# Summing keys and values over eight tokens by accumulating transfers, in a pooled-attention and gated feed-forward kernel

## The chip, the cores and the metric

The kernel runs on one core of a Trainium2 chip. The metric is the device time of one execution in microseconds, the median of three runs; lower is better. Five engines matter here: TensorE (PE, with its weight loads as PEld), VectorE (DVE), ScalarE (ACT), GpSimd (POOL) and the queue of SyncE (SP), from which the kernel before issues all its transfers.

## The reference

Inputs q, k, v are 8 batches x 8 heads x 576 tokens x 64. Keys and values are averaged over groups of eight tokens, so that 72 pooled keys and values remain for each head. Attention over them is followed by a gated feed-forward block on the 4608 tokens.

```python
k_p = k.reshape(B, H, Sp, pool, D).mean(axis=3)        # Sp = 72, pool = 8
v_p = v.reshape(B, H, Sp, pool, D).mean(axis=3)
scores = scale * np.matmul(q, k_p.transpose(0, 1, 3, 2))
scores = scores - np.max(scores, axis=-1, keepdims=True)
attn = np.exp(scores)
attn = attn / (np.sum(attn, axis=-1, keepdims=True) + 1e-09)
attn_out = np.matmul(attn, v_p)
x = attn_out.transpose(0, 2, 1, 3).reshape(B * S, H * D)   # 4608 x 512
out = ((x @ w_a) * (x @ w_b)) @ w_out                      # d_ff = 1536
```

## The kernel before

Every product is made of three matmuls on a high and a low part of its operands (`hi x hi + hi x lo + lo x hi`). ACT makes the high part by a rounding copy, and DVE or POOL the low part by a subtraction (`low_part`, line 182). So the feed-forward block alone has 9 token tiles x 12 slices of d_ff x 36 matmuls of 128x512.

The order of all work is written out when the program is built. The list `order` of `in` slices (`ffn_in`: 24 matmuls into psa and psb) and `out` slices (`ffn_out`: 12 matmuls into acc) is the backbone. Everything else runs in chains (Python generators) that `Chains.step` resumes: once in six backbone matmuls the clock of the chains moves by one step, and a chain that says `yield n` goes on n steps later. Each engine then executes its instructions strictly in the order in which the chains issued them, and waits for what the next one needs. Before the first backbone matmul, and wherever `need` is called, the steps go by without matmuls, so there they are no measure of time.

The chains: `load_keys(b)` and `load_values(b)` make the pooled keys `kdiag` and values `vdiag`, `vrem` of batch b; `chunk(i)` takes 128 (or 64) tokens through scores (`psc`), softmax (`s`, `m`, `z`), the split of the probabilities (`pr`, `rem`), their transposes (`ptr`) and the product with the values (`po`), which ends as `xh`, `xl`, the input of the backbone; `convert_weights` turns the float64 words of the three weight matrices into float32 (ACT lines 224 and 225, DVE lines 226, 230 and 235, with one area of loaded words for each matrix); `split_weight` makes the parts `jha/jla`, `jhb/jlb`, `jho/jlo` of a weight slice, in two buffers each; `gated` multiplies psa's copy `h` with psb (line 556) and splits the product into `hh`, `hl`.

In `load_keys` of batches 1 to 7 four transfers of 128x576 come on SP's queue, two at a time into two buffers, and four DVE reductions (line 281) sum groups of eight neighbours into `kp`, two after each pair of loads. ACT scales a pair into the high part of `kdiag` (line 292) and DVE makes its low part (line 297). `load_values` does the same with four transfers of 128x512 and two of 96x512 and six reductions (line 333) into `vp`; then come `vwide` (line 342), the low part of `vdiag` (line 356) and that of `vrem`. Batch 0 uses other buffers, loaded at the very start. POOL's work is the low parts of most weight slices and of the probabilities, and the division of the exponentials (line 457).

Of the kernel before, what the change touches and what calls it, by code (L numbers as in the profile page):

```python
# [9 lines left out]
F32 = mybir.dt.float32  # L10
# [16 lines left out]
NK = DM // P  # L27
# [19 lines left out]
NR = 3 * 4 * KR  # L47
NG = H // 4
# [70 lines left out]


@with_exitstack
def attn_moe_kernel(ctx: ExitStack, tc: tile.TileContext, q, k, v, vr, wa, wb, wo, out):
    nc = tc.nc
    const = ctx.enter_context(tc.tile_pool(name="const", bufs=1))
    sb = ctx.enter_context(tc.tile_pool(name="sb", bufs=2))
# [55 lines left out]
    def low_part(eng, lo, src, hi):  # L181
        eng.tensor_tensor(out=lo, in0=src, in1=hi.bitcast(F32), op=ALU.subtract)  # L182
# [72 lines left out]
    def split_weight(name, x):  # L255
# [7 lines left out]
        low_part(nc.vector if x < NF and name != "o" else nc.gpsimd, lo, raw[name][:, f, :], hi)  # L263
        parts[name, x] = hi, lo

    def load_keys(b):
        kd = kdiag[b % 2]
        kp = tmp(f"kp_{b}")[:, :NK * SP].rearrange("p (g s) -> p g s", g=NK)
        for g0 in range(0, NK, 2):
            gs = slice(g0, g0 + 2)  # L270
            if b == 0:
                kraw = [early_k[:, g, :] for g in (g0, g0 + 1)]
            else:
                if g0:
                    yield from wait(("kraw", b, 0))
                kraw = [sb.tile([P, S], F32, tag="kv", name=f"kraw_{b}_{g}") for g in (g0, g0 + 1)]
                for j in range(2):
                    nc.sync.dma_start(kraw[j], k[b, :, g0 + j, :])
                yield 4
            for j in range(2):  # L280
                nc.vector.tensor_reduce(
                    out=kp[:, g0 + j, :],
                    in_=kraw[j].rearrange("p (s j) -> p s j", j=POOL),
                    axis=AX.X,
                    op=ALU.add,
                )
                if b:
                    yield 1
            mark("kraw", b, g0)
            for e in range(2):  # L290
                r = slice(e * D, e * D + D)
                nc.scalar.mul(kd[r, gs, 0, e, :], kp[r, gs], 1.0 / POOL)
            if b:
                yield 1
            for e in range(2):
                r = slice(e * D, e * D + D)
                nc.vector.scalar_tensor_tensor(
                    out=kd[r, gs, 1, e, :],
                    in0=kp[r, gs],
                    scalar=1.0 / POOL,  # L300
                    in1=kd[r, gs, 0, e, :].bitcast(F32),
                    op0=ALU.mult,
                    op1=ALU.subtract,
                )
            mark("keys", b, g0)

    def load_values(b):
        vd = vdiag[b % 2]
        vrem = sb.tile([P, NG, 2, 2, D], F32R, tag="vrem", name=f"vrem_{b}")
        yield from wait(("keys", b, 2), ("values", b - 1))  # L310
        vp = sb.tile([P, NK + NG, D], F32, tag="vp", name=f"vp_{b}", bufs=1)
        for x0 in range(0, NK + NG, 2):
            if b == 0:
                vraw = [early_v[:, x, :] if x < NK else early_vr[:, x - NK, :] for x in (x0, x0 + 1)]
            else:
                if x0:
                    yield from wait(("vraw", b, x0 - 2))
                vraw = [sb.tile([P, S], F32, tag="kv", name=f"vraw_{b}_{x0 + j}")[:, :D * POOL] for j in range(2)]
                for j in range(2):
# [5 lines left out]
            for j in range(2):
                x, rows = x0 + j, P if x0 < NK else NR
                vv = vraw[j][:rows].rearrange("p (d j) -> p d j", j=POOL)
                if b == 0 and 0 < x < NK:
                    for n in (4, 2, 1):
                        to = vp[:rows, x].unsqueeze(2) if n == 1 else vv[:, :, :n]  # L330
                        nc.gpsimd.tensor_tensor(out=to, in0=vv[:, :, :n], in1=vv[:, :, n:2 * n], op=ALU.add)
                else:
                    nc.vector.tensor_reduce(out=vp[:rows, x], in_=vv, axis=AX.X, op=ALU.add)
            mark("vraw", b, x0)
            yield 1
        for e in range(2):
            r = slice(e * KM, e * KM + KM)
            nc.scalar.mul(vd[r, :, 0, r], vp[r, :NK], 1.0 / POOL)

        wide = tmp(f"vwide_{b}").rearrange("p (r j e d) -> p r (j e) d", r=NG, j=2, e=2)  # L340
        for r in range(NG):
            nc.vector.scalar_tensor_tensor(
                out=wide[:NR, r],
                in0=vp[:NR, NK + r].unsqueeze(1).broadcast_to([NR, 4, D]),
                scalar=1.0 / POOL,
                in1=mask[:NR].unsqueeze(2).broadcast_to([NR, 4, D]),
                op0=ALU.mult,
                op1=ALU.mult,
            )
        wide = wide.rearrange("p r c d -> p (r c d)")  # L350
        vrf = vrem.rearrange("p r j e d -> p (r j e d)")
        yield 1
        nc.scalar.copy(vrf[:NR], wide[:NR])
        for e in range(2):
            r = slice(e * KM, e * KM + KM)
            nc.vector.scalar_tensor_tensor(
                out=vd[r, :, 1, r],
                in0=vp[r, :NK],
                scalar=1.0 / POOL,
                in1=vd[r, :, 0, r].bitcast(F32),  # L360
                op0=ALU.mult,
                op1=ALU.subtract,
            )
# [298 lines left out]
    for kind, t, f, *_ in order:  # L662
        x = t * NF + f
# [7 lines left out]
    with tc.manual_schedule():  # L671
        load_early()
        nc.vector.tensor_copy(ident, ident0)
        for t in kdiag + vdiag:
            nc.gpsimd.memset(t.bitcast(F32), 0.0)
        nc.vector.tensor_reduce(
            out=mask[:NR], in_=ident0[:NR, :NR].rearrange("p (a c s) -> p c a s", a=3, c=4), axis=AX.XY, op=ALU.add
        )
        chains.start(load_keys(0), KEYS)
        for i in range(early):  # L680
            chains.start(chunk(i), (CHUNKS[0], i), EARLY_GAP * i)
        for i in range(early, sum(t < 2 for t in tile_of)):
# [16 lines left out]
        for n, (kind, t, f, *_) in enumerate(order):  # L699
            x = t * NF + f  # L700
# [82 lines left out]
```

## Time and profile before

| | us |
|---|---|
| median of the three runs | 1086.49 (1084.5 to 1088.29) |
| the profiled execution | 1083.36 |
| its span, first to last instruction | 1081.6 |
| PE busy in the span | 1032.1 (95%) |
| DVE busy | 585.9 (54%) |
| ACT busy | 515.6 (48%) |
| POOL busy | 506.6 (47%) |
| mean share of the DMA engines on SP's queue | 18.1% |

The profiled execution is 3.1 us faster than the median of the runs. The busy shares are means over two very different stages: a start of about 135 us, in which the first chunks and the first weight slices are made, and the long rest, in which the backbone runs. A busy PE in this profile includes matmuls that overlap, so 95% does not say that the array works at its peak.

### The profile page before, as it was taken

Reading aid. Unit: us, or ns where it says so; the run is one execution under the profiler, and the core shown is the slowest. Engines: PE = TensorE matmul, PEld = TensorE weight load, DVE = VectorE, ACT = ScalarE, POOL = GpSimd, SP = SyncE. Lnnn points to the kernel's source line nnn. Section 1 sums busy time; section 2 is a strip of 40 time slices with the busy share of each in tenths; the row PEclk is TensorE's granted clock in tenths of the full one; section 3 lists DMA queues with packets and bytes.
Section 4 is the critical chain, followed back from the end, with each engine's and each line's share of the span. In section 5 each row is a group of like instructions: output and inputs, shape, how many; then the busy total and the mean of one; then the engine's idle time right before and its main releaser. Section 6 shows DMA issues by size and latency. Waiting matters only on the chain.

```text
span 1081.6 us, 13576 instructions
## 1 busy us (share of the span) xinstructions
PE 1032.1 (95%) x4964; PEld 855.9 (79%) x4964; DVE 585.9 (54%) x941; ACT 515.6 (48%) x1035; POOL 506.6 (47%) x425
## 2 busy tenths in 40 slices
PE   4569999999999999999999999999999999999998
PEld 4457788788878888888877888888887888888886
DVE  8879967845784347534575437543567344322112
ACT  4656645454554445444544445444543444443332
POOL 6322200055565555555546545554545455554442
PEclk9769999999999999999999999999999999999999
DMA  6335445221330004000320003100220010001001
GB/s 221 105 120 157 147 137 170 93 90 50 115 110 1 1 23 140 14 1 1 96 90 1 1 5 106 45 1 1 93 83 1 1 59 1 1 1 39 1 1 39
DMA packets 32178, 63.79 MB, mean 59 GB/s; under 512 B 7376, under 2 KB 7376, under 8 KB 32112
## 3 DMA queue, kind: packets, MB, share of 16 engines
q1 hardware_dynamic: 32112, 62.93, 18.1%
q8 instruction: 39, 0.64, 0.3%
q14 instruction: 27, 0.22, 0.1%
HBM read 51.38 MB, written 11.53 MB: 58 GB/s over the span
## 4 chain that ended last, share of the span: by engine, by line
PE 85%; DVE 9%; ACT 3%; issue 2%; DMA 1%; POOL 0%; DVEq 0%; ACTq 0%; POOLq 0%
PE psb L599 9%; PE psa L599 9%; PE acc L621 9%; PE psb L601 9%; PE psb L600 8%; PE psa L601 8%; PE psa L600 8%; PE acc L623 8%; PE acc L622 8%; PE ptr L502 2%; PE psc L431 2%; PE psc L417 1%; PE po L539 1%; PE po L540 1%; PE po L538 1%
## 5 line engine op out<-in xcount | busy, mean ns | idle before, releaser
L556 DVE TENSOR_TENSOR h<-psb,h 128x512 f32<-128x512 f32 x108 | 74.6, 691 | 318.7 <-PE psb L601 312.8
L182 POOL TENSOR_TENSOR jlb<-wb_raw,jhb 128x512 fp32r<-128x512 f32 x88 | 115.1, 1307 | 254.6 <-ACT jhb L261 254.6
L182 POOL TENSOR_TENSOR jlo<-wo_raw,jho 128x512 fp32r<-128x512 f32 x108 | 143.1, 1325 | 122.5 <-ACT jho L261 122.5
L606 ACT COPY h<-psa 128x512 f32<-128x512 f32 x108 | 63.5, 588 | 251.8 <-PE psa L601 239.8
L599 PE MATMUL psa<-xh,jha 128*128 128x512 f32 x432 | 173.7, 402 | 0.0
L599 PE MATMUL psb<-xh,jhb 128*128 128x512 f32 x432 | 172.0, 398 | 0.8 <-DVE h L556 0.8
L621 PE MATMUL acc<-jho,hh 128*128 128x512 f32 x432 | 171.6, 397 | 0.0
L600 PE MATMUL psa<-xl,jha 128*128 128x512 f32 x432 | 169.4, 392 | 0.7 <-DVE xl L182 0.7
L601 PE MATMUL psa<-xh,jla 128*128 128x512 f32 x432 | 169.7, 393 | 0.4 <-DVE jla L182 0.4
L601 PE MATMUL psb<-xh,jlb 128*128 128x512 f32 x432 | 168.8, 391 | 0.0
L600 PE MATMUL psb<-xl,jhb 128*128 128x512 f32 x432 | 168.7, 391 | 0.0
L623 PE MATMUL acc<-jho,hl 128*128 128x512 f32 x432 | 168.6, 390 | 0.0
L622 PE MATMUL acc<-jlo,hh 128*128 128x512 f32 x432 | 168.2, 389 | 0.0
L182 POOL TENSOR_TENSOR jla<-wa_raw,jha 128x512 fp32r<-128x512 f32 x88 | 120.6, 1371 | 73.9 <-ACT jha L261 66.6
L182 DVE TENSOR_TENSOR hl<-h,hh 128x512 fp32r<-128x512 f32 x100 | 92.7, 927 | 33.5 <-ACT hh L569 33.3
L569 ACT CAST hh<-h 128x512 fp32r<-128x512 f32 x100 | 62.2, 622 | 95.1 <-DVE h L556 92.5
L601 PEld LDWEIGHTS psa<-xh,jla 128*128 128x128 f32 x432 | 81.8, 189 | 18.5 <-DVE jla L182 0.8
L601 PEld LDWEIGHTS psb<-xh,jlb 128*128 128x128 f32 x432 | 81.2, 188 | 17.4
L623 PEld LDWEIGHTS acc<-jho,hl 128*128 128x128 f32 x432 | 81.1, 188 | 17.5
L599 PEld LDWEIGHTS psb<-xh,jhb 128*128 128x128 f32 x432 | 81.3, 188 | 16.4 <-DVE h L556 1.2
L600 PEld LDWEIGHTS psa<-xl,jha 128*128 128x128 f32 x432 | 82.0, 190 | 15.6 <-DVE xl L182 1.1
L599 PEld LDWEIGHTS psa<-xh,jha 128*128 128x128 f32 x432 | 81.7, 189 | 14.8
(93 smaller groups left out, 1693.4 us busy)
## 6 DMA issues: line engine op xcount, KB each, us to landing
out<-y SPq DMA_DIRECT2D x36, 256.0 KB, 2.2
kraw<-in_k SPq DMA_DIRECT2D x28, 288.0 KB, 4.1
qraw<-in_q SPq DMA_DIRECT2D x28, 256.0 KB, 3.7
vraw<-in_v SPq DMA_DIRECT2D x28, 256.0 KB, 3.1
words<-in_wa SPq DMA_DIRECT2D x12, 512.0 KB, 3.6
words<-in_wb SPq DMA_DIRECT2D x12, 512.0 KB, 3.5
words<-in_wo SPq DMA_DIRECT2D x12, 512.0 KB, 3.6
vraw<-in_vr SPq DMA_DIRECT2D x14, 192.0 KB, 2.6
```

Source lines behind the costliest of these rows:

```text
L182: eng.tensor_tensor(out=lo, in0=src, in1=hi.bitcast(F32), op=ALU.subtract)
L431: nc.tensor.matmul(pt[:n, :2 * hk], qh[:, g, :n], kd[:, g].rearrange("p w e s -> p (w e s)"), start=True, stop=False)
L502: nc.tensor.transpose(ptr[:rows, g, :n], src, ident[:n, :n])
L556: nc.vector.tensor_tensor(out=h, in0=pt, in1=h, op=ALU.mult)
L569: nc.scalar.copy(hh, h)
L599: nc.tensor.matmul(pt, wh[:, c], xh[:, kk], start=(kk == 0), stop=False)
L600: nc.tensor.matmul(pt, wh[:, c], xl[:, kk], start=False, stop=False)
L601: nc.tensor.matmul(pt, wl[:, c], xh[:, kk], start=False, stop=(kk == NK - 1))
L606: nc.scalar.copy(h, pt)
L621: nc.tensor.matmul(acc[c], hh[:, cs], wh, start=first, stop=False)
L622: nc.tensor.matmul(acc[c], hh[:, cs], wl, start=False, stop=False)
L623: nc.tensor.matmul(acc[c], hl[:, cs], wh, start=False, stop=last)
```

## The change

Keys and values of batches 1 to 7 are laid out on the host as four pieces with two summands side by side in each row: `kj` has pieces of 128 x 2 x 288 and `vj` of 128 x 2 x 384 (the last two head groups of the values padded with zeros to 128 rows). One plain transfer on SP's queue brings the first piece. Three transfers issued from POOL's queue add the other three to it on their way into the same tile, each three steps after the one before it. Each of them waits until the one before has landed. One DVE addition then sums the two halves. The reductions, the small tiles, `vp` and the shared load buffers `kv` go; `kraw` and `vraw` become one tile each. `load_values` no longer waits for the keys before it begins to load, and its work behind the sum stands elsewhere by some steps. The high and low parts of the keys are made for all four head groups at once. `load_keys(1)` starts at step 4 and not 8.

```diff
+GATHER_FIRST, GATHER = 3, 3
-EARLY_GAP, VALUES_START, KEYS_START, WEIGHTS_START, CONVERT_AFTER = 1, 2, 8, 10, 5
+EARLY_GAP, VALUES_START, KEYS_START, WEIGHTS_START, CONVERT_AFTER = 1, 2, 4, 10, 5
...
+    def gather(dst, src, apart):
+        nc.sync.dma_start(dst, src[0])
+        for x in range(1, POOL // 2):
+            yield apart
+            nc.gpsimd.dma_start(dst, src[x], accum_op=ALU.add)
+        yield apart
+        nc.vector.tensor_tensor(out=dst[:, 0], in0=dst[:, 0], in1=dst[:, 1], op=ALU.add)
...
     def load_keys(b):
...
+            yield from wait(("keys", b - 1, 2))
+            kraw = sb.tile([P, 2, NK * SP], F32, tag="kraw", name=f"kraw_{b}", bufs=1)
+            yield from gather(kraw, kj[b - 1].rearrange("x p (j c) -> x p j c", j=2), GATHER_FIRST if b == 1 else GATHER)
+            kp = kraw[:, 0].rearrange("p (g s) -> p g s", g=NK)
...
-                kraw = [sb.tile([P, S], F32, tag="kv", name=f"kraw_{b}_{g}") for g in (g0, g0 + 1)]
-                for j in range(2):
-                    nc.sync.dma_start(kraw[j], k[b, :, g0 + j, :])
-                yield 4
-            for j in range(2):
-                nc.vector.tensor_reduce(out=kp[:, g0 + j, :], ...)
...
     def load_values(b):
-        yield from wait(("keys", b, 2), ("values", b - 1))
+        yield from wait(("values", b - 1))
+        vraw = sb.tile([P, 2, (NK + NG) * D], F32, tag="vraw", name=f"vraw_{b}", bufs=1)
+        vp = vraw[:, 0].rearrange("p (x d) -> p x d", d=D)
+            yield from gather(vraw, vj[b - 1].rearrange("x p (j c) -> x p j c", j=2), GATHER_FIRST if b == 1 else GATHER)
...
-                    if x0 < NK:
-                        nc.sync.dma_start(vraw[j], v[b, :, x0 + j, :])
-                    else:
-                        nc.sync.dma_start(vraw[j][:NR], vr[b, :, x0 + j - NK, :])
-                yield 3
...
+        yield from wait(("keys", b, 2))
```

TensorE's instructions stand in the same order before and after, without an exception. The order moves on DVE, ACT, POOL and SP. Three places follow.

DVE in the start, from the first chunks' division to the first chunk of batch 1; `kp`, `kraw` and `kdiag_76` belong to the keys of batch 1, `wa` and `wb` to the first weight slices. Before:

```order
L281 TENSOR_REDUCE kp_219<-kraw_0_220 128x72
L457 TENSOR_TENSOR s_235<-s_235,z_237 128x576
L281 TENSOR_REDUCE kp_219<-kraw_1_221 128x72
L226 TENSOR_SCALAR wa_raw<-wa_raw 128x512
L297 SCALAR_TENSOR_TENSOR kdiag_76<-kp_219,kdiag_76 64x2x72 x2
L230 SCALAR_TENSOR_TENSOR wa_raw<-words,wa_raw 128x512
L235 ISA wa_raw<-wa_raw,wlow_a_332 128x1024
L182 TENSOR_TENSOR xl_343<-po_0_349,xh_342 128x2x256
```

And now, with the sum of the keys (line 275) behind the conversion of the first slice; the sum of the values follows some fifteen rows later:

```order
L459 TENSOR_TENSOR s_234<-s_234,z_236 128x576
L228 TENSOR_SCALAR wa_raw<-wa_raw 128x512
L232 SCALAR_TENSOR_TENSOR wa_raw<-words,wa_raw 128x512
L237 ISA wa_raw<-wa_raw,wlow_a_331 128x1024
L275 TENSOR_TENSOR kraw_170<-kraw_170 128x288
L184 TENSOR_TENSOR xl_337<-po_0_344,xh_336 128x2x256
```

Two reductions and a pair of `kdiag` rows are gone from in front of the first conversion, and an addition that needs the third accumulating transfer stands behind it.

POOL in the start, from the split of the first chunks' queries (`ql`) to the first chunk of batch 1 (`s_395`). Before:

```order
L182 TENSOR_TENSOR ql_187<-wa_raw,qh_186 128x512
L182 TENSOR_TENSOR pr_202<-s_120,pr_202 128x512
L182 TENSOR_TENSOR rem_203<-s_120,rem_203 128x2x32
L182 TENSOR_TENSOR pr_211<-s_139,pr_211 128x512
L182 TENSOR_TENSOR rem_212<-s_139,rem_212 128x2x32
L457 TENSOR_TENSOR s_216<-s_216,z_218 128x576
L182 TENSOR_TENSOR pr_304<-s_216,pr_304 128x512
L182 TENSOR_TENSOR rem_305<-s_216,rem_305 128x2x32
L182 TENSOR_TENSOR pr_327<-s_235,pr_327 128x512
```

And now:

```order
L273 DMA kraw_170<-in_kj 128x576
L184 TENSOR_TENSOR pr_205<-s_120,pr_205 128x512
L184 TENSOR_TENSOR rem_206<-s_120,rem_206 128x2x32
L184 TENSOR_TENSOR pr_215<-s_139,pr_215 128x512
L184 TENSOR_TENSOR rem_216<-s_139,rem_216 128x2x32
L273 DMA kraw_170<-in_kj 128x576
L459 TENSOR_TENSOR s_220<-s_220,z_222 128x576
L273 DMA vraw_237<-in_vj 128x768
L273 DMA kraw_170<-in_kj 128x576
L184 TENSOR_TENSOR pr_305<-s_220,pr_305 128x512
L184 TENSOR_TENSOR rem_306<-s_220,rem_306 128x2x32
L273 DMA vraw_237<-in_vj 128x768
```

Six accumulating transfers stand between the splits of the first four chunks' probabilities (the last `vraw` follows behind the fourth chunk's), and each holds what is behind it on POOL until the one before it of the same tile has landed.

DVE in the long stage, where the values of batch 5 meet a chunk's scores (`s` from `psc`, line 437); the same pattern returns at batch 7. Before:

```order
L333 TENSOR_REDUCE vp_5007<-vraw_4_5137 96x64
L333 TENSOR_REDUCE vp_5007<-vraw_5_5138 96x64
L342 SCALAR_TENSOR_TENSOR vwide_5190<-vp_5007,mask 96x256 x2
L556 TENSOR_TENSOR h_5171<-psb_3_5173,h_5171 128x512
L356 SCALAR_TENSOR_TENSOR vdiag_78<-vp_5007,vdiag_78 64x4x64 x2
L182 TENSOR_TENSOR vrem_5006<-vwide_5190,vrem_5006 32x512
L437 TENSOR_REDUCE s_5185<-psc_0_5237 64x144
L437 TENSOR_REDUCE s_5185<-psc_1_5241 64x144
L182 TENSOR_TENSOR hl_5232<-h_5171,hh_5231 128x512
```

And now:

```order
L275 TENSOR_TENSOR vraw_4900<-vraw_4900 128x384
L558 TENSOR_TENSOR h_5052<-psb_3_5054,h_5052 128x512
L344 SCALAR_TENSOR_TENSOR vwide_5089<-vraw_4900,mask 96x256 x2
L358 SCALAR_TENSOR_TENSOR vdiag_78<-vraw_4900,vdiag_78 64x4x64 x2
L439 TENSOR_REDUCE s_5064<-psc_0_5116 64x144
L439 TENSOR_REDUCE s_5064<-psc_1_5120 64x144
L184 TENSOR_TENSOR hl_5109<-h_5052,hh_5108 128x512
L184 TENSOR_TENSOR vrem_4899<-vwide_5089,vrem_4899 32x512
```

The low part of `vrem` went from in front of the first scores to behind them, and two reductions became one addition. At the values of batch 3 the two `vdiag` rows moved in the same way, from between the two pairs of scores to behind both.

More of the change, by code (lines that the diff above doesn't have):

```diff
@@ L121, in attn_moe_kernel @@
 @with_exitstack
-def attn_moe_kernel(ctx: ExitStack, tc: tile.TileContext, q, k, v, vr, wa, wb, wo, out):
+def attn_moe_kernel(ctx: ExitStack, tc: tile.TileContext, q, k, v, vr, kj, vj, wa, wb, wo, out):
     nc = tc.nc
@@ L264, in split_weight @@
         parts[name, x] = hi, lo
+    def gather(dst, src, apart):
[5 more added lines that the diff above has]
+        nc.vector.tensor_tensor(out=dst[:, 0], in0=dst[:, 0], in1=dst[:, 1], op=ALU.add)
     def load_keys(b):
         kd = kdiag[b % 2]
-        kp = tmp(f"kp_{b}")[:, :NK * SP].rearrange("p (g s) -> p g s", g=NK)
-        for g0 in range(0, NK, 2):
-            gs = slice(g0, g0 + 2)
-            if b == 0:
-                kraw = [early_k[:, g, :] for g in (g0, g0 + 1)]
-            else:
-                if g0:
-                    yield from wait(("kraw", b, 0))
-                kraw = [sb.tile([P, S], F32, tag="kv", name=f"kraw_{b}_{g}") for g in (g0, g0 + 1)]
-                for j in range(2):
-                    nc.sync.dma_start(kraw[j], k[b, :, g0 + j, :])
-                yield 4
-            for j in range(2):
[L281 to L289, printed above, removed]
+        if b == 0:
+            kp = tmp(f"kp_{b}")[:, :NK * SP].rearrange("p (g s) -> p g s", g=NK)
+        else:
+            yield from wait(("keys", b - 1, 2))
+            kraw = sb.tile([P, 2, NK * SP], F32, tag="kraw", name=f"kraw_{b}", bufs=1)
+            yield from gather(kraw, kj[b - 1].rearrange("x p (j c) -> x p j c", j=2), GATHER_FIRST if b == 1 else GATHER)
+            kp = kraw[:, 0].rearrange("p (g s) -> p g s", g=NK)
+            yield 1
+        many = 2 if b == 0 else NK
+        for g0 in range(0, NK, many):
+            gs = slice(g0, g0 + many)
+            if b == 0:
+                for g in range(g0, g0 + many):
+                    nc.vector.tensor_reduce(
+                        out=kp[:, g, :],
+                        in_=early_k[:, g, :].rearrange("p (s j) -> p s j", j=POOL),
+                        axis=AX.X,
+                        op=ALU.add,
+                    )
             for e in range(2):
@@ L304, in load_keys @@
                 )
-            mark("keys", b, g0)
+            for g in range(g0, g0 + many, 2):
+                mark("keys", b, g)
     def load_values(b):
@@ L309, in load_values @@
         vrem = sb.tile([P, NG, 2, 2, D], F32R, tag="vrem", name=f"vrem_{b}")
-        yield from wait(("keys", b, 2), ("values", b - 1))
[L311 to L319, printed above, removed]
-                    if x0 < NK:
-                        nc.sync.dma_start(vraw[j], v[b, :, x0 + j, :])
-                    else:
-                        nc.sync.dma_start(vraw[j][:NR], vr[b, :, x0 + j - NK, :])
-                yield 3
[L325 to L328, printed above, removed]
+        yield from wait(("values", b - 1))
+        vraw = sb.tile([P, 2, (NK + NG) * D], F32, tag="vraw", name=f"vraw_{b}", bufs=1)
+        vp = vraw[:, 0].rearrange("p (x d) -> p x d", d=D)
+        if b:
+            yield from gather(vraw, vj[b - 1].rearrange("x p (j c) -> x p j c", j=2), GATHER_FIRST if b == 1 else GATHER)
+            yield 1
+        else:
+            for x in range(NK + NG):
+                vv = (early_v[:, x, :] if x < NK else early_vr[:NR, x - NK, :]).rearrange("p (d j) -> p d j", j=POOL)
+                rows = P if x < NK else NR
+                if 0 < x < NK:
                     for n in (4, 2, 1):
@@ L333, in load_values @@
                     nc.vector.tensor_reduce(out=vp[:rows, x], in_=vv, axis=AX.X, op=ALU.add)
-            mark("vraw", b, x0)
-            yield 1
+                if x % 2:
+                    yield 1
+        yield from wait(("keys", b, 2))
         for e in range(2):
@@ L761 @@
     vrl = np.ascontiguousarray(np.repeat(vrl, 3, axis=1).reshape(B, NR, NG, D * POOL))
+    kj = kl[1:].reshape(B - 1, P, NK, SP, POOL // 2, 2).transpose(0, 4, 1, 5, 2, 3)
+    kj = np.ascontiguousarray(kj.reshape(B - 1, POOL // 2, P, 2 * NK * SP))
+    vj = np.zeros((B - 1, P, NK + NG, D, POOL), v.dtype)
+    vj[:, :, :NK] = vl[1:].reshape(B - 1, P, NK, D, POOL)
+    vj[:, :NR, NK:] = vrl[1:].reshape(B - 1, NR, NG, D, POOL)
+    vj = vj.reshape(B - 1, P, NK + NG, D, POOL // 2, 2).transpose(0, 4, 1, 5, 2, 3)
+    vj = np.ascontiguousarray(vj.reshape(B - 1, POOL // 2, P, 2 * (NK + NG) * D))
     wl = {
@@ L769 @@
     wol = np.ascontiguousarray(inputs["moe_w_out"].reshape(NF, P, DM).transpose(1, 0, 2)).view(np.int64)
-    host = {"q": ql, "k": kl, "v": vl, "vr": vrl, "wa": wl["a"], "wb": wl["b"], "wo": wol}
+    host = {"q": ql, "k": kl[:1], "v": vl[:1], "vr": vrl[:1], "kj": kj, "vj": vj, "wa": wl["a"], "wb": wl["b"], "wo": wol}
     nc = bacc.Bacc("TRN2", target_bir_lowering=False, num_devices=1, dynamic_dma_scratch_size=2048)
```

## Prediction

> **What bounds the kernel now.** I read the page first, then the busy time by stretches, then who waits for whom on TensorE, and last the chain and the timelines of the places found. The page's first line, and the stretches; columns there: length, PE busy (count), PEld, DVE, ACT, POOL, granted clock, DMA share, GB/s.
>
> ```profile
> span 1081.6 us, 13576 instructions
> ```
>
> ```profile
> 0.00:54.00 54.00, 29.11 (x144) 25.71 (x144) 45.08 (x84) 27.62 (x62) 27.09 (x37) 0.88 0.50 163
> 54.00:91.00 37.00, 27.97 (x123) 21.67 (x124) 31.27 (x55) 23.34 (x49) 7.13 (x8) 0.71 0.44 133
> 91.00:135.00 44.00, 40.62 (x206) 31.87 (x205) 40.79 (x68) 29.16 (x58) 11.70 (x9) 1.00 0.48 149
> 135.00:1060.00 925.00, 917.29 (x4420) 762.85 (x4419) 464.57 (x731) 430.23 (x859) 456.81 (x370) 1.00 0.14 46
> ```
>
> There are two kernels in this. Up to 91 us TensorE is idle for 34 of 91 us, while DVE is busy for 76 of them (84%): DVE is the busiest engine there. From 135 us on TensorE is idle for 7.7 us of 925, and DVE is busy for half the time. A shorter DVE list can gain in the start, and behind it no more than those 7.7 us, which are few single waits (engine, line, waited for: us, times, longest; from 135 us on):
>
> ```profile
> PE psc L431 <- DVE s L437: 5.1, 4, 1.4
> PE ptr L502 <- DVE s L437: 1.9, 1, 1.9
> PE psb L599 <- DVE h L556: 0.8, 1, 0.8
> ```
>
> Since TensorE's order is unchanged, the change can act on the time only through waits.
>
> **The change part by part: the start.** The chain there (start, us, what), and the same place in DVE's and ACT's timelines:
>
> ```profile
> 29.96 0.62 DVE kp L281
> 32.31 0.67 DVE kp L281
> ...
> 37.87 0.69 DVE wa_raw L235
> 42.36 0.66 DVE kp L281
> 43.93 0.66 DVE kp L281
> ```
>
> ```profile
> 33.01 0.65 ACT L292 ACTIVATE kdiag<-kp 64x144 fp32r<-64x144 f32 x2 [1.89 <-DVE kp L281]
> 36.27 0.74 DVE L297 SCALAR_TENSOR_TENSOR kdiag<-kp,kdiag 64x144 fp32r<-64x144 f32 x2
> ```
>
> All four key reductions of batch 1 are on the chain: 0.62 + 0.67 + 0.66 + 0.66 = 2.6 us go. The kdiag work stays (two wider pairs for four), so I count it at nothing on balance, as the same elements on the same engines. The addition of 128x288 that comes in has no row; the nearest are a subtraction of 128x256 and the 0.7 us of 128x512 operations:
>
> ```profile
> L182 DVE TENSOR_TENSOR ql<-qraw,qh 128x256 fp32r<-128x256 f32 x8 | 3.4, 422 | 0.0
> ```
>
> I take 0.45 us for it and 0.55 us for the 128x384 of the values (bounds 0.4 and 0.7). So the keys give 2.6 - 0.45 = 2.1 us.
>
> The values of batch 1 cost DVE six reductions and five later operations:
>
> ```profile
> 53.51 1.27 DVE L333 TENSOR_REDUCE vp<-vraw 128x64 f32<-128x512 f32 x2
> ...
> 69.96 1.26 DVE L333 TENSOR_REDUCE vp<-vraw 128x64 f32<-128x512 f32 x2
> 81.53 1.27 DVE L333 TENSOR_REDUCE vp<-vraw 96x64 f32<-96x512 f32 x2
> 84.98 0.75 DVE L342 SCALAR_TENSOR_TENSOR vwide<-vp,mask 96x256 f32<-96x256 f32 x2
> 87.92 0.84 DVE L356 SCALAR_TENSOR_TENSOR vdiag<-vp,vdiag 64x256 fp32r<-64x256 f32 x2
> 90.56 0.68 DVE L182 TENSOR_TENSOR vrem<-vwide,vrem 32x512 fp32r<-32x512 f32 x1
> ```
>
> The last three rows (2.3 us) move forward to about 46 to 52 us, and the sum of 0.55 us with them; the pair of reductions at 53.5 (1.2 us) goes. So DVE has about 1.6 us more before 54 us and 1.2 + 1.2 + 2.3 = 4.7 us less in 54 to 91. How much of the 4.7 reaches the end? There the chain also runs through the loads of words:
>
> ```profile
> 78.36 3.42 DMA words<-in_wa
> ```
>
> With its two successors (3.46 each, at 84 and 90 us) that is 10.3 us of the 37 that no shorter DVE list touches; each next load is issued behind DVE's line 230, though, so a shorter list brings it forward. I take two thirds of 4.7, 3.1 us. (Bounds: nothing, and all.) The 1.6 us stand at 46 to 54 us, where DVE waits for ACT and TensorE anyway; I take half, 0.8 us. Start without new waits: 2.1 + 3.1 - 0.8 = 4.4 us gained.
>
> **What the start has to wait for.** DVE's two additions need the third accumulating transfer, and POOL's queue holds each transfer until the one before has landed. POOL's own rows (start, us) say where it has room:
>
> ```profile
> 18.62 1.45 POOL L182 TENSOR_TENSOR ql<-wa_raw,qh 128x512 fp32r<-128x512 f32 x1
> ...
> 24.79 0.32 POOL L182 TENSOR_TENSOR rem<-s,rem 128x64 fp32r<-128x64 f32 x1
> 28.55 1.15 POOL L457 TENSOR_TENSOR s<-s,z 128x576 f32<-128x576 f32 x1 [3.44 <-DVE z L455]
> ...
> 47.61 1.15 POOL L457 TENSOR_TENSOR s<-s,z 64x576 f32<-64x576 f32 x1 [11.08 <-DVE z L455]
> ```
>
> No transfer of before accumulates or is issued from POOL. Nearest rows for L, the time from issue to landing (KB each and median; then the smallest, median and largest of the key loads, from the view of that tile):
>
> ```profile
> kraw<-in_k SPq DMA_DIRECT2D x28, 288.0 KB, 4.1
> words<-in_wa SPq DMA_DIRECT2D x12, 512.0 KB, 3.6
> ...
> DMA to landing us min/median/max: 2.7/4.1/8.6
> ```
>
> Size hardly counts (512 KB take no longer than 288 KB), so that an accumulating transfer, which also has to read its destination, need not be dearer for its bytes. I take the median of the same size, 4.1, and add 0.7 us for an issue from POOL (below: nothing; above: one of POOL's own 1.3 us operations): L = 4.8, POOL blocked for 1.0 us at each issue. Bounds of L: 2.7 and 8.6.
>
> In the Trainium skill, "DMA: Bandwidth & Descriptors", section "Anatomy of one DMA", a transfer from GpSimd takes about 2.0 us plus its bytes at 436 GB/s, 2.7 us for a piece of the keys; by that L would be under 4, no addition would wait, and the time would be 1078.
>
> With L = 4.8 the keys' transfers go out at 20.1 (behind ql), 25.1 (behind the second rem) and 30.7 (behind s at 28.55 and the first values' transfer), and land by 35.5. DVE comes to their sum at 38.56, the end of line 235, less the 1.3 us of two reductions, 0.65 of ACT's kdiag and 0.74 of DVE's, so 35.9: no wait. The values' transfers go out at 29.7, 34.5 and 39.3 and land at 44.1; DVE comes to that sum at about 43.6. It waits 0.5 us. On POOL the first four chunks' low parts come up to 1.5 us later; that is covered by the gaps shown (3.44 us, 11.08 us) and by TensorE's later use. Start: 4.4 - 0.5 = 3.9 us gained.
>
> **The long stage.** The five rows of DVE behind its waits:
>
> ```profile
> 196.37 1.27 DVE L333 TENSOR_REDUCE vp<-vraw 128x64 f32<-128x512 f32 x2
> 307.35 2.74 DVE L356 SCALAR_TENSOR_TENSOR vdiag<-vp,vdiag 64x256 fp32r<-64x256 f32 x2 [0.92 <-ACT vdiag L338]
> ...
> 554.28 1.27 DVE L333 TENSOR_REDUCE vp<-vraw 96x64 f32<-96x512 f32 x2 [2.22 <-DMA vraw<-in_vr]
> 559.14 1.77 DVE L182 TENSOR_TENSOR vrem<-vwide,vrem 32x512 fp32r<-32x512 f32 x1
> 569.20 3.84 DVE L182 TENSOR_TENSOR hl<-h,hh 128x512 fp32r<-128x512 f32 x1 [0.69 <-ACT hh L569]
> ```
>
> The reductions at 196.37 stood ahead of h and go: the 0.8 us wait goes. The vdiag rows at 307.35 now stand behind the scores that TensorE waits for: 1.9 go. At batch 5 (and 7) vrem, 1.77, is behind the first scores, and 1.27 of reductions became 0.55: that exceeds the wait of 1.4, which goes twice, 2.8 in all. The other two of the four waits, (5.1 - 2.8) / 2 = 1.1 each, stand behind an hl of 3.84 us that the change does not touch; they stay. Gain: 0.8 + 1.9 + 2.8 = 5.5 us.
>
> New waits: 36 transfers hold POOL for 1.0 us each and up to L - 4.1 = 0.7 more, since three steps are 18 backbone matmuls at the pace of the first row below, 4.1 us. Who waits for POOL there has room of 2.6 us at a chunk (the low part ends, TensorE uses it), and least at the end of tile 1, 0.46 us:
>
> ```profile
> 128.77 0.23 PE psa L599
> ```
>
> ```profile
> 641.87 1.29 POOL L182 TENSOR_TENSOR pr<-s,pr 128x512 fp32r<-128x512 f32 x1 [0.73 <-ACT pr L466]
> 645.80 0.47 PE L502 MATMUL ptr<-ident,pr 128*128 128x128 f32 x4
> ...
> 297.54 1.79 POOL L182 TENSOR_TENSOR jlo<-wo_raw,jho 128x512 fp32r<-128x512 f32 x1 [1.41 <-ACT jho L261]
> ...
> 299.79 0.39 PE L622 MATMUL acc<-jlo,hh 128*128 128x512 f32 x1
> ```
>
> 1.7 us stay under 2.6 at a chunk. At the end of tile 1 two of batch 3's transfers stand in front of such a jlo; I charge both with 1.7 - 0.5 = 1.2, 2.4 us together (bounds: nothing, for the 1.41 us gap covers most of one; and 1.7 at each of some nine tight places, 15 us). Long stage: 5.5 - 2.4 = 3.1 us gained. SP's queue issues 42 fewer transfers; nothing on TensorE waited for them in the waits shown, so I count that at nothing.
>
> **Sum.** 3.9 + 3.1 = 7.0 us. The profiled execution, 1083.4 us, would become 1076.4; the runs' median stands 3.1 above it, and 1086.5 - 7.0 = 1079.5.
>
> **The rivals.**
>
> *Slow landings (slower).* If an accumulating transfer takes more than about 5.7 us, each link of the three lengthens the sum's wait: at L = 6 the keys land at 38.1, 2.2 us after DVE wants them, and the values at 47.7, with DVE then at 45.8, 1.9 more; the start gains 0.3. In the long stage the third transfer holds POOL by 2 x 1.9 + 1.0 = 4.8 us, over the 2.6 of a chunk at six places where a transfer stands between s and pr: 13 us lost, 5.5 gained, 1094 in all; with half of those places covered by POOL's gaps, 1087, no change. For it: DVE's busy queue has in-order waits, and the largest landing is 8.6 in the crowded first 27 us. Against: the medians, 3.6 and 4.1. It decides from L = 5.7 on. The Trainium skill, "SBUF — State Buffer", section "Who interferes with whom", has a mechanism that leads there: transfers issued from GpSimd lack their descriptors while DVE runs in a two-port mode. No row of the trace of before can show it.
>
> *The gain stays hidden (no change).* If the loads of words and ACT set the pace of 54 to 91 us, the start gains only the keys' 2.1 less the 0.8, and if two of the 1.4 to 1.9 us waits return elsewhere in DVE's list, the long stage gains nothing: about 1085. For it: 10.3 of 37 us of the chain are those loads. Against: DVE is busy for 31 of the 37.
>
> *More than forecast.* L below 4.3, all 4.7 us on the path, no new wait in the long stage: 2.1 + 4.7 - 0.8 + 5.5 = 11.5, 1075.
>
> **How the numbers follow.** Forecast (1077 to 1083) 0.47, more than forecast 0.13, hidden gain 0.22, slow landings 0.18. A measurement of this kernel tells 0.3%, 3.3 us, from no change. Forecast and more than forecast are faster by more than that, 0.6; the hidden gain is no change, 0.22; the slow landings are slower, 0.18. The range 1072 to 1090 takes in all cases but the worse half of the slow landings and the extremes; given that it is faster, 1074 to 1082.
>
> **What would show it.** Right: TensorE's idle time to 91 us falls from 34 by about 4 us; the waits of psc and ptr on s L437 fall from 7.0 to about 2.2 us; DVE's busy time falls by some 38 us (70 reductions of about 0.65 against 14 additions of about 0.5); the accumulating transfers land within 4 to 5.5 us. Wrong: DVE idle in front of the additions in the start for more than 2 us, waits of TensorE on jlo, jla, jlb or pr in the long stage, or a POOL that waits for transfers through whole tiles. The forecast fails first if L is over 5.7 us.

## The result, and the profile after

The changed kernel takes 1114.26 us (median of four runs, 1111.23 to 1115.9), the kernel before beside it 1086.63 us: a ratio of 1.0256, 95% interval 1.0235 to 1.0276. It is 28 us slower; the forecast was 1079.5, with 1090 as its upper end. The profiled execution took 1114.63 us. Its page: the span, the engines, the chain of waits by engine, and two rows of the DMA issues (KB each, median us from issue to landing).

```profile
span 1112.9 us, 13482 instructions
...
PE 1040.6 (94%) x4964; PEld 861.2 (77%) x4964; DVE 551.5 (50%) x871; ACT 512.8 (46%) x1021; POOL 543.4 (49%) x467
...
PE 74%; DVE 9%; DMA 7%; issue 4%; POOL 3%; ACT 3%; SPq 0%; DVEq 0%; POOLq 0%; ACTq 0%
...
vraw<-in_vj POOLq DMA_DIRECT2D x21, 384.0 KB, 5.0
...
kraw<-in_kj POOLq DMA_DIRECT2D x21, 288.0 KB, 4.5
```

DVE's list is shorter by 34 us (585.9 to 551.5; some 38 were forecast), and POOL's longer by 37 (42 issues of 0.87, where 1.0 each was charged). But transfers now hold 7% of the chain that ended last. The stretches (columns as in the prediction):

```profile
0.00:54.00 54.00, 24.46 (x120) 21.67 (x120) 41.83 (x73) 24.63 (x54) 28.75 (x40) 1.00 0.72 188
54.00:91.00 37.00, 27.91 (x124) 22.21 (x124) 29.13 (x53) 22.83 (x49) 10.88 (x10) 0.82 0.29 85
...
135.00:1060.00 925.00, 898.54 (x4298) 745.15 (x4297) 429.94 (x668) 418.99 (x831) 473.05 (x394) 0.99 0.19 47
```

TensorE's idle time up to 91 us rose from 33.9 to 38.6 us, and in the long stage, where 7.7 us of waits were all that could be won, from 7.7 to 26.5. Most of the loss is there. Who waits for whom in it (us, times, longest):

```profile
DVE vraw L275 <- DMA vraw<-in_vj: 31.0, 6, 7.6
POOL vraw L273 <- DMA vraw<-in_vj: 23.3, 8, 4.6
...
POOL kraw L273 <- DMA kraw<-in_kj: 20.7, 8, 6.4
...
PE psc L433 <- DVE s L439: 18.3, 6, 4.8
DVE kraw L275 <- DMA kraw<-in_kj: 17.9, 6, 4.4
ACT kdiag L300 <- DVE kraw L275: 17.3, 5, 4.8
```

DVE stands 48.9 us in front of its twelve additions, 4.1 us at each in the mean, and POOL 44 us in front of its transfers. TensorE's wait for `s` (psc, 5.1 us before) is 18.3. ACT hands on the waits at the keys' sums: it stands 17.3 us in front of `kdiag`, and what is behind it in its order comes late to TensorE (`jhb` by 0.9 us at 197 us, `jho` by 1.4 at 296, `pr` by 2.5 at 696). One batch shows how they hang together, first POOL's three transfers, then DVE, then TensorE:

```profile
435.06 0.84 POOL L273 DMA_DIRECT2D vraw<-in_vj  x1
...
440.47 0.90 POOL L273 DMA_DIRECT2D vraw<-in_vj  x1 [1.98 <-DMA vraw<-in_vj]
...
446.07 0.89 POOL L273 DMA_DIRECT2D vraw<-in_vj  x1 [3.37 <-DMA vraw<-in_vj]
```

```profile
445.64 0.69 DVE L184 TENSOR_TENSOR hl<-h,hh 128x512 fp32r<-128x512 f32 x1 [0.69 <-ACT hh L571]
452.54 0.56 DVE L275 TENSOR_TENSOR vraw<-vraw 128x384 f32<-128x384 f32 x1 [6.21 <-DMA vraw<-in_vj]
453.02 0.81 DVE L439 TENSOR_REDUCE s<-psc 128x144 f32<-128x288 f32 x2
```

```profile
453.52 0.61 PE L433 MATMUL psc<-kdiag,qh 128*128 128x288 f32 x1 [4.79 <-DVE s L439]
```

The transfers follow each other every 5.4 to 5.6 us, not every 4.1 (three steps), since each waits for the landing before it. The third, with a landing of 6.45 us, is there 17 us after the first was issued, and DVE after 11. Over the twelve sums these two times are 17.1 and 13.1 us in the mean, and DVE's lies between 7.6 and 17.3. The evacuation of the scores (line 439: DVE reads them out of `psc`, so that TensorE can write there again), which has nothing to do with the values, stands behind the sum and TensorE behind that.

### The profile page after: what moved, and what is told of

The parts are those of the page before. It is cut to its first block, busy times and chain, and to the rows that moved or that the text cites. A ratio compares the mean times of both kernels' runs of the same rounds, so it can differ in the third digit from the quotient of the medians.

```text
span 1112.9 us, 13482 instructions
## 1 busy us (share of the span) xinstructions
PE 1040.6 (94%) x4964; PEld 861.2 (77%) x4964; DVE 551.5 (50%) x871; ACT 512.8 (46%) x1021; POOL 543.4 (49%) x467
## 4 chain that ended last, share of the span: by engine, by line
PE 74%; DVE 9%; DMA 7%; issue 4%; POOL 3%; ACT 3%; SPq 0%; DVEq 0%; POOLq 0%; ACTq 0%
PE psb L601 8%; PE psa L601 8%; PE acc L623 7%; PE psb L602 7%; PE psb L603 7%; PE acc L624 7%; PE psa L602 7%; PE psa L603 7%; PE acc L625 7%; DMA vraw<-in_vj 5%; PE ptr L504 2%; PE psc L433 2%; DVE z L455 1%; POOL jlo L184 1%; POOL s L459 1%
## 5 line engine op out<-in xcount | busy, mean ns | idle before, releaser
L184 POOL TENSOR_TENSOR jlb<-wb_raw,jhb 128x512 fp32r<-128x512 f32 x88 | 118.1, 1342 | 227.1 <-ACT jhb L263 227.0
L184 POOL TENSOR_TENSOR jlo<-wo_raw,jho 128x512 fp32r<-128x512 f32 x108 | 145.4, 1346 | 97.2 <-ACT jho L263 97.2
L184 POOL TENSOR_TENSOR jla<-wa_raw,jha 128x512 fp32r<-128x512 f32 x88 | 122.9, 1397 | 71.2 <-ACT jha L263 67.9
L184 DVE TENSOR_TENSOR hl<-h,hh 128x512 fp32r<-128x512 f32 x100 | 95.7, 957 | 34.9 <-ACT hh L571 34.7
L601 PEld LDWEIGHTS psb<-xh,jhb 128*128 128x128 f32 x432 | 82.0, 190 | 17.3 <-ACT jhb L263 1.3
L623 PEld LDWEIGHTS acc<-jho,hh 128*128 128x128 f32 x432 | 81.4, 188 | 16.8 <-ACT jho L263 1.8
```

The costliest lines, as they stand in the source:

```text
L601: nc.tensor.matmul(pt, wh[:, c], xh[:, kk], start=(kk == 0), stop=False)
L623: nc.tensor.matmul(acc[c], hh[:, cs], wh, start=first, stop=False)
```

## The experiments

All medians stand beside runs of the kernel before on the same chip (1085.5 to 1086.2 us); the ratio is to those. Four theories: A, DVE's own in-order wait for the third landing holds TensorE; B, POOL, held between transfers, makes the low parts of weights and probabilities late; C, the loss is in the start; and, formed after the first four runs, D.

**The sum alone later.**

```diff
-GATHER_FIRST, GATHER = 3, 3
+GATHER_FIRST, GATHER, SUM_LATER = 3, 3, 6
-        yield apart
+        yield apart + late      # SUM_LATER for batches 2 to 7
         nc.vector.tensor_tensor(out=dst[:, 0], ...)
```

> Only VectorE's addition (and what follows it) of batches 2 to 7 is put six steps, some 8 us, later; the transfers stand where they did, so POOL waits between them as before. Theory A (VectorE, held in order in front of the addition until the third transfer has landed, holds TensorE): the waits before L275 (52 us in the changed kernel) shrink to the 3 us of batch 1, TensorE's idle times of 2 to 5 us in the long stage go, and with them the stretches at half clock: 18 + 5 = 23 us back, so 1091 us (1087 to 1096). Theory B (POOL, held 50 us between transfers and 37 us issuing, makes the low parts jlo and pr late): at most 2 us back, 1112 us or more. Theory C (the loss is in the start, in the order of batch 1's work): 1114 us.

1097.15 us, ratio 1.0109 (1.0093 to 1.0125). DVE's waits in front of the additions are gone in the long stage, and 17 us came back, not 23. What stayed is not B's either: in the long stage TensorE waits four times, 13.6 us in all, each time for the same line 439 and never for a weight's low part or `pr`. At two of the four places, of 2.0 and 2.4 us, what DVE does ahead of it is this (DVE and POOL at the values of batch 4, then TensorE):

```profile
431.20 4.69 DVE L184 TENSOR_TENSOR hl<-h,hh 128x512 fp32r<-128x512 f32 x1 [0.69 <-ACT hh L571]
```

```profile
430.68 0.89 POOL L273 DMA_DIRECT2D vraw<-in_vj  x1 [4.54 <-DMA vraw<-in_vj]
431.28 1.60 POOL L184 TENSOR_TENSOR jlb<-wb_raw,jhb 128x512 fp32r<-128x512 f32 x1
432.53 1.59 POOL L184 TENSOR_TENSOR jlo<-wo_raw,jho 128x512 fp32r<-128x512 f32 x1
433.78 1.56 POOL L184 TENSOR_TENSOR jla<-wa_raw,jha 128x512 fp32r<-128x512 f32 x1
```

```profile
436.32 0.40 PE L433 MATMUL psc<-kdiag,qh 128*128 128x288 f32 x1 [2.02 <-DVE s L439]
```

POOL waited 4.5 us for a landing, three low parts piled up, and it worked them off without a gap. Beside that train DVE's `hl`, which takes 0.69 us elsewhere, took 4.69 and ended 0.5 us behind it. This is theory D: a POOL that is held piles up work, and the train holds DVE. The Trainium skill, "SBUF — State Buffer", section "Who interferes with whom", says that a VectorE instruction with two operands in SBUF contends with a GpSimd instruction that reads SBUF, and that whichever issues first blocks the other. The trace agrees, and goes further: `hl` waited for the whole train, not for one instruction of it. DVE's operations that run over 0.8 us longer than the shortest quarter of their form are 39.1 us too long in all after 135 us in the kernel before, 43.8 in the changed kernel, and 62.6 here.

The other two places, of 4.6 us each (batches 5 and 7), are not D's: POOL had waited for no landing there, and the train is one that the kernel before has too (569.20 in the prediction's rows). The late sum put the values' work into it and in front of the scores:

```profile
571.25 4.68 DVE L344 SCALAR_TENSOR_TENSOR vwide<-vraw,mask 96x256 f32<-96x256 f32 x2
575.86 0.98 DVE L358 SCALAR_TENSOR_TENSOR vdiag<-vraw,vdiag 64x256 fp32r<-64x256 f32 x2
576.88 0.69 DVE L184 TENSOR_TENSOR hl<-h,hh 128x512 fp32r<-128x512 f32 x1
577.60 1.63 DVE L184 TENSOR_TENSOR vrem<-vwide,vrem 32x512 fp32r<-32x512 f32 x1
```

So this run moved two things. Matched matmul by matmul with the spaced kernel below (TensorE's order is the same in all kernels, so each matmul has its twin), D's two places make TensorE 8 us later, and the two places of the late sum 10.

**The transfers spaced.** GATHER from 3 to 6 steps, KEYS_AHEAD from 18 to 30, VALUES_AFTER from 16 to 28.

> The transfers of batches 2 to 7 stand six steps apart (8.2 us) where they stood three, and their chains start 12 steps earlier, so that neither POOL has to wait for the transfer before nor VectorE for the third. Theory A: as with the late sum alone, 1091 us (1087 to 1096). Theory B: 1092 us or less, and at least 15 us below the kernel with the late sum alone. If both VectorE's and POOL's waits cost, it is lower than the late sum alone by TensorE's waits for jlo and pr, 3 to 6 us. Theory C: 1114 us.

1079.85 us, ratio 0.9947 (0.9933 to 0.9962): faster than both kernels. (More exactly: the keys' chain begins 12 steps earlier and its sum stays; the values' chain begins at the same step and its sum comes 12 steps later.) It is 17 us below the late sum alone, more than the 3 to 6 of A with B, and as much as B alone had asked for; but B is ruled out by the run above, where TensorE waited for none of what POOL makes. The sums stand elsewhere here too, so some 10 of the 17 us are their places. After 135 us no addition and no transfer is shown waiting for a landing, and TensorE idles 2.5 us in the long stage:

```profile
135.00:1060.00 925.00, 922.55 (x4449) 768.57 (x4448) 439.06 (x675) 429.68 (x852) 486.37 (x408) 1.00 0.19 47
```

**Batch 1 by reductions as before**, alone (first text) and with the late sum (second); its raw keys and values land in parts of the weights' buffers that are still free:

```diff
-        if b == 0:            # in load_keys; load_values alike
+        if b < 2:
...
+            for g in range(NK):
+                nc.sync.dma_start(second_k[:, g, :], k[1, :, g, :])
```

> Batch 1 alone is reduced by VectorE as in the kernel before (its raw keys and values land in parts of the weights' buffers that are still free), batches 2 to 7 are gathered as in the changed kernel. By the delay of TensorE's matmuls, which stood at 4.4 us when the start was over (58 us), the start's share is 4 us: 1110 us (1107 to 1112). By the prediction, which gave the start a gain of 3.9 us, it is 1118 us. Theory A and B both leave the long stage as it is.

> Late sum for batches 2 to 7 and batch 1 reduced as before, together. Theory A with the start's share: 1114 - 23 - 4 = 1087 us, and 1083 if the 3 us that the long stage waited for the reductions in the kernel before are then gained. Theory B: 1108 us.

1111.29 us (ratio 1.0243, 1.0225 to 1.0262) and 1097.52 (1.0097, 1.0072 to 1.0121). Alone it gains 3 us, the size that C gave to the start; beside the late sum it gains nothing (A had asked for 1087 or less, B for 1108). The 3 us are no sign of C: TensorE idles 38.2 us of the first 91 in that kernel, as in the changed one (38.6), so the start was not given back, and the gain comes later. What limits C is the spaced kernel: TensorE idles 38.9 us in its start, and it is faster than the kernel before all the same.

**Only POOL's order clumped.** In the spaced kernel, GATHER back to 3 and the sums 12 steps late, so that TensorE, DVE, ACT and SP keep the spaced kernel's instructions in the spaced kernel's order.

> As the spaced kernel (1079.9 us), except that the second and third transfer of POOL follow three steps apart again, as in the changed kernel: TensorE, VectorE, ScalarE and SyncE have the same instructions in the same order as in the spaced kernel, and the additions stand at its places; only POOL's order differs. Theory D (a POOL that waits for a landing piles up its low parts, works them off without a gap, and VectorE's operations with two operands in SBUF cannot start beside that train, so that TensorE waits): POOL waits 40 us for DMAs again, VectorE's operations are stretched by some 15 us more than in the spaced kernel, and the time is 1092 to 1098 us. Theory A alone (only VectorE's own wait for the landing costs, and the late sum alone kept 17 us because its addition stood at a poor place): 1080 us.

1084.74 us, ratio 0.9982 (0.9966 to 0.9997). POOL waits 41.0 us for landings again, DVE's operations are 59.8 us too long against 48.7 in the spaced kernel, and the median is 4.9 us higher (runs from 1079.9 to 1087.6; by the means 3.9). D is at work here, since nothing but POOL's order differs and TensorE waits only for line 439; but it costs 4 to 5 us, not the 12 to 18 forecast, which took the two places of the late sum for D's. How much depends on what stands behind the held operation: of its trains only two meet an evacuation that TensorE waits for (1.93 us at 687 us, behind an `hl` of 4.60, and 1.21 at 774).

**Four steps apart**, sums as in the spaced kernel (GATHER 4, KEYS_AHEAD 22, VALUES_AFTER 28).

> As the spaced kernel, except that the transfers stand four steps (5.5 us) apart, the additions at the same places. Theory A and D: what decides is whether a step of the spacing is longer than issue and landing together (0.9 + 4.5 or 5.0 us from the traces). At 5.5 us it nearly covers them, so POOL waits under 10 us in all and the time is 1080 to 1084 us. If instead the chip wants transfers far apart for some other reason (transfers of SyncE beside them), it lies half way, 1087 us.

1092.15 us, ratio 1.0059 (1.0042 to 1.0076): worse than three steps with the same sums. POOL still waits 39 us for landings, not under 10. Distance alone is not it. At 570 us, DVE and POOL:

```profile
569.79 6.21 DVE L184 TENSOR_TENSOR hl<-h,hh 128x512 fp32r<-128x512 f32 x1 [0.69 <-ACT hh L571]
```

```profile
569.31 1.28 POOL L184 TENSOR_TENSOR jlb<-wb_raw,jhb 128x512 fp32r<-128x512 f32 x1
570.56 1.28 POOL L184 TENSOR_TENSOR jlo<-wo_raw,jho 128x512 fp32r<-128x512 f32 x1
571.79 0.87 POOL L273 DMA_DIRECT2D vraw<-in_vj  x1
572.40 1.56 POOL L184 TENSOR_TENSOR pr<-s,pr 64x512 fp32r<-64x512 f32 x1
573.63 0.60 POOL L184 TENSOR_TENSOR rem<-s,rem 64x64 fp32r<-64x64 f32 x1
573.91 1.53 POOL L184 TENSOR_TENSOR jla<-wa_raw,jha 128x512 fp32r<-128x512 f32 x1
```

The train was there before (569.20 in the prediction's rows: `hl` 3.84 us, the two waits of 1.1 us that were to stay). The issue of one transfer makes it 0.6 us longer, `jla` then follows without a gap, and `hl` waits for `jla` too. TensorE waits 3.49 us there and 3.48 at the same place of batch 7 (834.7 us).

**Five steps apart** (GATHER 5, KEYS_AHEAD 26), and then, from four steps, **two of the 42 transfers three places earlier on POOL** (the values' third of batches 5 and 7, ahead of `s`, in POOL's idle time):

> As the kernel with four steps (1092.2 us), with five steps (6.9 us) between the transfers; additions, TensorE, VectorE and ScalarE stand in the same order again. In the kernel with four steps the values' third transfer of batches 5 and 7 stands inside a train of POOL's low parts (jlb, jlo, transfer, pr, rem, jla without a gap), VectorE's hl beside it takes 6.2 us and TensorE waits 3.5 us, twice. With five steps that transfer stands ahead of jlb, outside the train. Theory D: hl there falls to the 3.9 us of the kernel before and TensorE's waits there to 1.1 us, which with the slow stretches behind them is 4 us each: 1092 - 8 = 1084 us or a little less, as POOL waits less for landings too. If only the distance counted (POOL's waits for landings, 39 us at four steps), the time would go in proportion to those waits, to 1083 to 1086 us, but hl would still take over 5 us.

> The kernel with four steps (1092.2 us) with two of its 42 accumulating transfers moved: the values' third transfer of batches 5 and 7 stands three places earlier in POOL's order, ahead of s, jlb and jlo, where POOL had 3.7 us of idle time in front of s. Everything else, on every engine, keeps its order. Five steps had put that transfer behind s, where it still made POOL's train 0.6 us longer, so that jla joined it and hl was held until 575 us as before. Theory D: POOL's train from jlb to rem ends in front of jla again, hl takes 3.9 us instead of 6.2, TensorE waits 1.1 us instead of 3.5 and keeps its full clock, at both places: 1092.2 - 2 x 4 = 1084 us (1083 to 1086). If it is not the train: 1092 us.

Five steps: 1088.45 us, ratio 1.0016 (1.0005 to 1.0027), where 1084 was forecast. I had the transfer's place wrong: between `s` and `jlb` it still makes the train late by 0.6 us, `hl` stayed at 6.19 us, and TensorE's two waits at 3.47 and 3.48. POOL's waits for landings fell to 4.6 us, so those do not set the time here.

Two transfers moved: 1088.53 us, ratio 1.0025 (1.0003 to 1.0046), over a wide spread of 1081.8 to 1094.2, where 1083 to 1086 was forecast. At both places the trace, of the execution that took 1081.8 us, shows the waits as forecast:

```profile
567.04 3.99 DVE L184 TENSOR_TENSOR hl<-h,hh 128x512 fp32r<-128x512 f32 x1 [0.69 <-ACT hh L571]
570.96 1.76 DVE L439 TENSOR_REDUCE s<-psc 64x144 f32<-64x288 f32 x4
```

```profile
571.45 0.34 PE L433 MATMUL psc<-kdiag,qh 128*64 128x288 f32 x1 [1.27 <-DVE s L439]
```

TensorE waits 1.27 and 1.44 us instead of 3.49 and 3.48, and its clock stays full. In this one trace, matched matmul by matmul with the one of four steps, the two places give back 4.7 and 3.5 us. The median moved by less, 3.6 us. Six executions, those from 1089.95 us up, have a granted clock of 0.978 to 0.980, the other six 0.982 to 0.992; why it differs, and with it the spread, is open.

**Plain transfers.** The changed kernel with `accum_op` left out, at the same places: each transfer overwrites the one before, and the sum over eight is left out.

> The changed kernel with POOL's transfers plain instead of accumulating, so that each overwrites the one before and the sum over eight is left out: same places, same bytes, same waits. It measures what accumulation adds to the 4.5 and 5.0 us from issue to landing. If a plain transfer lands within 3.2 us (the step of 4.1 us less POOL's 0.9), the waits before L275 and L273 go with no instruction moved, and the time falls to 1083 to 1090 us. If the landing is not made by accumulating, it stays at 1112 to 1116 us.

1084.67 us, ratio 0.9988 (0.9978 to 0.9997). Landings, and what remains of the waits after 135 us:

```profile
vraw<-in_vj POOLq DMA_DIRECT2D x21, 384.0 KB, 3.5
...
kraw<-in_kj POOLq DMA_DIRECT2D x21, 288.0 KB, 3.2
```

```profile
POOL vraw L273 <- DMA vraw<-in_vj: 13.6, 6, 3.2
POOL kraw L273 <- DMA kraw<-in_kj: 13.6, 4, 6.4
DVE vraw L275 <- DMA vraw<-in_vj: 11.3, 5, 3.3
...
DVE kraw L275 <- DMA kraw<-in_kj: 3.5, 2, 2.6
```

No instruction moved; each landing is 1.3 to 1.5 us shorter and each issue 0.55 us instead of 0.87, and 29.6 us of 1114.3 are gone. DVE's waits fell from 48.9 to 14.8 us. That makes 4 us and more over the three links of a chain; a sum waited 4.1 us in the mean of the 12 in the changed kernel and 1.2 here. So the length of the landings makes the loss, and not the places of the transfers alone. What is left of the waits is mostly POOL's: at the keys of batch 3, for one, it issues the third transfer 8 us after the second has landed.

**The start.** The spaced kernel with batch 1 by reductions and batch 0's values behind its keys as before; and the spaced kernel with KEYS_START 2 and GATHER_FIRST 2.

> The spaced transfers for batches 2 to 7, with batch 1 reduced as in the kernel before and the values of batch 0 again behind its keys: the start as before, the long stage as in the spaced kernel. The spaced kernel still entered the long stage 1.9 to 3.5 us behind the kernel before: with the start given back, 1077 us (1075 to 1079). If the delay is not the start's, 1080 us.

> The spaced kernel (1079.9 us) with batch 1's chain begun two steps earlier and its transfers two steps apart, so that POOL issues the three of the keys before the third block's s, pr and rem. In the spaced kernel the third of the keys stood in front of pr, waited 1.8 us for the landing before, and TensorE was 3.5 us behind the kernel before when the long stage began; with plain transfers it was 2 us ahead of it. If POOL's order in the start makes that delay: 1076 to 1078 us. If it is the landing itself (keys needed before they are there): 1080 us or more.

1080.59 us (ratio 0.9947, 0.9933 to 0.9962) and 1085.61 (1.0000, 0.9989 to 1.0010): neither gains. In the first, TensorE still idles 38.5 of the first 91 us; what of this is my buffers' loads and what the later first matmul of that execution (8.46 us against 6.91) stays open. The second is the main error once more, made by me: with the transfers the sum moved forward too.

```profile
34.82 0.46 DVE L275 TENSOR_TENSOR kraw<-kraw 128x288 f32<-128x288 f32 x1 [5.69 <-DMA kraw<-in_kj]
```

The third transfer was issued at 26.19 and the sum could start at 34.82. DVE stood 5.7 us, and TensorE 9.0 behind it.

## Why the prediction was wrong, by its own steps

**The step that failed is "New waits" of the long stage.** It charged the lateness L - 4.1 = 0.7 us of a transfer to POOL alone, once for each transfer, and asked only who waits for POOL. It did not follow the third transfer to the addition, as the same prediction had done for the start. Each link's lateness adds up to the sum, which DVE takes in order, with an evacuation behind it that TensorE waits for. By its own L = 4.8 and its own step of 4.1 us, three links are at least 14.4 us against 12.3: a wait of 2.1 us at each of 12 sums. Measured: 4.1 in the mean. From the first issue to the sum it took 17.1 us: 14.9 for three landings (some took 6 to 7.6 us, so that the mean lies above the medians), 0.35 between a landing and the next issue wherever POOL stood waiting for it, and, at four of the sums, 1.5 to 7.4 us because POOL came late to the issue. DVE was there after 13.1. The step also left out ACT, which waits for the keys' sums in its own order.

**L was right, its threshold was not.** L = 4.8 was forecast; 4.5 and 5.0 are the medians. The rival of slow landings came nearest to the mechanism (in the start it lets every link lengthen the sum's wait) and was given 0.18, because it was to decide from L = 5.7 on, by POOL's 2.6 us of room at a chunk. By the links, and with a POOL that comes in time, it decides where 3 x L and some 0.7 us between them exceed 12.3 us, near L = 3.9; this is an estimate from the two kernels' rows. The plain transfers at 3.2 and 3.5 lie under it, and that kernel's time is the time before (ratio 0.9988); the accumulating ones lie 0.6 and 1.1 above it and cost 28 us. The forecast of L came out right by two errors: accumulation, taken to cost nothing, costs 1.3 to 1.5 us, and a plain transfer from POOL lands sooner than the 4.1 us of SyncE's loads that the 0.7 was added to.

**The waits that were to go went.** With the landings out of the way, in the spaced kernel, TensorE's idle time in the long stage is 2.5 us instead of 7.7: 5.3 us, where 5.5 were forecast, with the two waits of 1.16 us left behind an `hl` of 3.88 us, much as said. In the changed kernel itself they were buried. That the spaced kernel's 1079.85 is the forecast's 1079.5 is luck: its start has 5 us more idle time where 3.9 were to be gained.

**The start.** Forecast: 3.9 us gained, with L = 4.8 and no wait at the keys. Measured: 4.7 us more idle time, of which 1.3 are there at the first matmul (8.18 us against 6.91), before any of POOL's transfers. POOL's rows and DVE's:

```profile
34.68 0.87 POOL L273 DMA_DIRECT2D kraw<-in_kj  x1 [2.31 <-DMA kraw<-in_kj]
35.24 1.62 POOL L184 TENSOR_TENSOR pr<-s,pr 128x512 fp32r<-128x512 f32 x1
...
44.43 0.88 POOL L273 DMA_DIRECT2D vraw<-in_vj  x1 [4.00 <-DMA vraw<-in_vj]
```

```profile
35.12 2.30 DVE L232 SCALAR_TENSOR_TENSOR wa_raw<-words,wa_raw 128x512 int32<-128x512 int32 x1
37.56 2.71 DVE L237 CUSTOM_DVE_ANT_0 wa_raw<-wa_raw,wlow_a 128x1024 uint16<-128x1024 uint16 x1
...
52.12 0.56 DVE L275 TENSOR_TENSOR vraw<-vraw 128x384 f32<-128x384 f32 x1 [3.19 <-DMA vraw<-in_vj]
```

The links are longer there (26.90 to 34.68 for the keys' second, 7.8 us; 44.43 to 52.12 for the values' third, 7.7). The keys' third transfer holds `pr` until 35.24, which was at 30.43, and the shifted `pr` and `rem` run beside DVE's conversions, which take 2.30 and 2.71 us instead of 0.69 each. "Covered by the gaps shown" was wrong. With plain transfers TensorE's idle time to 91 us is 31.7, 2.2 below the kernel before: so without the accumulation the forecast's sign holds.

**What was named as a sign against the forecast** came: DVE idle over 2 us before an addition in the start (3.2), and POOL waiting for transfers. TensorE's wait on `jlo` was 0.9 us and on `pr` 2.5; both stand behind ACT's wait for a sum of the keys, so they are A's, handed on by ACT, and no wait is shown that B alone made.

**The whole of the 31.3 us** between the two spans (1081.6 and 1112.9): TensorE is 4.3 us late where the long stage begins (135 us, matched matmul by matmul), idles 18.8 us more in it, and runs some 8 us late by half clock behind four of its pauses (next but one section).

## What to carry to other kernels

A chain of n dependent transfers needs n times the step from one issue to the next before its consumer's place in the consumer engine's order; what is missing is paid there, and by everything queued behind it, on that engine and on those that wait for it. So price the chain at the consumer and not at the link. A wait that is moved off one engine comes back in another shape: an engine that was held works off what has piled up in one train, and here POOL's train held DVE's subtractions. So space such transfers wider than that step (here 8.2 us against 5.4 to 5.6), keep their issues out of the trains in front of work that the bottleneck waits for, and place the consumer for itself: a consumer moved to a poor place cost 10 us here.

## What the runs showed of the hardware

An accumulating transfer from POOL costs 0.87 us of POOL and lands after 4.5 us (288 KB) or 5.0 (384 KB); a plain one from the same queue 0.55, 3.2 and 3.5.

TensorE's granted clock can halve behind a pause of a few microseconds (stretches of the changed kernel, behind pauses of 3.29, 2.63 and 4.79 us; the granted clock is the number behind the counts, and the pause of 2.63 left it at 1.00):

```profile
217.10:220.10 3.00, 2.98 (x9) 2.60 (x10) 1.73 (x5) 1.08 (x3) 0.00 (x0) 0.50 0.00 0
323.70:326.70 3.00, 2.92 (x17) 2.33 (x18) 2.71 (x7) 1.50 (x4) 0.80 (x1) 1.00 0.61 198
453.50:456.50 3.00, 2.98 (x9) 2.59 (x10) 2.93 (x7) 0.46 (x2) 0.00 (x0) 0.50 0.00 0
```

At half clock 9 matmuls pass in 3 us. Behind the pauses of 3.29, 4.79 and 3.65 us (the last at 715 us) this cost 1.3, 2.8 and 1.6 us on top of them (the growth of TensorE's lateness, matched matmul by matmul with the kernel before), and behind two short pauses close together, of 1.39 and 0.86 us at 296 and 297 us, 1.7 (granted clock 0.51 from 298.7 to 302.1 us). The Trainium skill, "TensorE: Matmul & The Clock Gate", section "What's actually happening", has TensorE fall to half clock after at least one idle window of about 3.4 us, in a window that runs freely. The trace agrees in the pauses of 3.65 and 4.79 us; but in the kernel with the late sum a pause of only 2.02 us (436.32 in the rows above) was followed by half clock as well:

```profile
438.00:440.00 2.00, 2.00 (x7) 1.52 (x6) 1.19 (x2) 0.26 (x1) 0.00 (x0) 0.50 0.00 0
```

So a pause shorter than the window can do it, though not every one does (the pause of 2.63 us above did not), and there the 2 us of waiting made the matmuls behind it 4.0 us later.
